# Reordering the transfers at the start of the second block, and the mirrored joins, in a fused Fourier mixing and squared-ReLU kernel

## The chip, the cores and the metric

The kernel runs on one core of one Trainium2 chip. A core has a matrix engine (TensorE, PE in the profile, with its weight loads listed as PEld), a vector engine (VectorE, DVE), a scalar engine (ScalarE, ACT), a general engine (GpSimd, POOL) and SP, which here only issues transfers (DMAs). Each engine works through its own list of instructions in order, and semaphores make one wait for another. The metric is the device time of one execution in microseconds (us), the median of several runs; lower is better.

## The reference

Two parts, both in float32. The first mixes a batch of 8 sequences of 3008 tokens with 256 features by a two-dimensional Fourier transform and keeps the real part. The second takes every token through two matrices with a squared ReLU between them.

```python
def _attn_ref(x):                       # x: (8, 3008, 256)
    X = np.fft.fft(x, axis=1)
    X = np.fft.fft(X, axis=2)
    return X.real.astype(np.float32)

def _moe_ref(x, w_in, w_out):           # x: (24064, 256), w_in: (256, 2048), w_out: (2048, 256)
    h = x @ w_in
    r = np.maximum(h, 0.0)
    g = r * r
    return (g @ w_out).astype(np.float32)
```

## The kernel before

**What is computed, and from what.** The transform over the tokens is done as products with tables of cosines and sines, after x has been folded (sums and differences of rows that share a table row). The result for one sequence is held as three pieces: P and Q, two arrays of 128 rows by 1505 columns (names `Pt` and `Qt`), and E, one row of 1505 numbers, the column of features that belongs to neither. The transform over the features is folded into the first matrix: G1 and G2 are w_in multiplied by the tables of that transform, `gE` the part of it that goes with E. So h = G1 P + gE E + G2 Q for one column and, with a minus in front of G2 Q, for its mirror image, which is why one step makes both.

**Steps and blocks.** The 1505 columns of a sequence are cut into six blocks of up to 252 columns, and the 2048 hidden features into 16 chunks, taken two at a time: eight steps to a block, 48 to a sequence, numbered through as `i`, with `j = i % 8`. A step is: products of G1 with P and G2 with Q on PE (`hP`, `hQ`, L1028; in steps 0 to 9 `ph`, L999 and L1001, one half of the step at a time); on VectorE E times gE added to hP (L1032; L1014 in steps 0 to 9), then sum and difference with hQ into `g` (L1036 and L1037; L1016 and L1017); on ScalarE ReLU (L1041) and square (L1044) in place. Two steps together then go through the second matrix by a scheme with fewer products: GpSimd makes sums of `g` (`s`, L1056 to L1073), and PE multiplies `g` and `s` with w_out and sums of it (`F` and `S`, L1093). The first block does the second product without that scheme (`mA`, `mB`, L1122). The sums of w_out (`wsum`) are made while steps 6 to 11 run: `copy_wout` has ScalarE copy a quarter into PSUM (`sw`, L397) and `sum_wout` has VectorE add from it (L404).

**The order.** Nothing is scheduled by a planner. Steps 0 to 9 run in the order of the tokens in ORDER, each a name for one piece of work: `f9a` are the products of step 9's first half, `d9a` the VectorE work on them, `rl` and `sq` the ReLU and square, `cm` the sums on GpSimd, `bk` the second product, `sc2b` and `su2b` the copy and the sums of one part of w_out, `PW`, `H`, `PR` the steps that bring a weight from float64 to float32. From step 10 on a loop does the same step by step; pieces of the next sequence's folding and transform are placed beside the steps, from step 12 on.

**The row of E and the transfers.** Each block needs its 252 values of E on all 128 partitions. For the first block a product spreads them (`spread_e`). For the second, token `spl` has GpSimd store the lower part of E to DRAM (`store_lower`, L989) and SP load it back, broadcast, as `ew` (`load_window`, L977). The upper part is stored by SP (`store_upper`, L992) once the mirrored joins of Q are done. `lc` issues column loads (`load_columns`, L470): single columns of x for sequences 1 to 7, from which GpSimd later makes the rows of E of those sequences; a bare `lc` issues four, `lc1` one. `load_later` issues the load of one x tile of a later sequence (`xt`, L183, or L174 in pieces of 32 rows); its first three stand in the code at the first `f` token of step 8. GpSimd takes the difference of the first two tiles at token `df` (L605), ahead of the sums of step 8. All transfers from SP go out in the order of the code, and an issue that waits holds those behind it.

**Mirrored joins.** P and Q of sequence 0 are joined from even and odd parts. The lower columns (0 to 752) are joined before and in the first block. The upper, mirrored columns come from four joins (`join_hi`; L801 for Q, L811 for P), which `rows_at(i)` places at the end of the steps from `HI_AT` on. Block three (columns 504 to 755), which starts at step 16, is the first that needs one of them. `load_window` for the third block stands at step `HI_AT + 2`.

**PSUM.** The tiles `ph`, `hP`, `hQ` and the scratch for folding (`sp`) share two buffers in turn, so a product can start only when the tile two before it has been read.

The lines of the loop that place the joins' companions:

```python
if (i == HI_AT + 2 or j == 2 and i > HI_AT) and i + NJ < len(steps):
    load_window(*steps[i - j + NJ][:3])
...
if HI_AT <= i < HI_AT + 4:
    rows_at(i)
```

Of the kernel before, what the change touches and what calls it, by code (L numbers as in the profile page):

```python
# [84 lines left out]
def kernel(  # L85
# [20 lines left out]
    NJ = NFC // 2  # L106
# [3 lines left out]
    NX = 3  # L110
# [59 lines left out]
    def load_x(b, t):  # L170
        if b and (t >= ODD0 or t == TWO + 1):
            xt[b, t] = xp.tile([P, 4, D], F32, name="xt", tag="x")
            for p, first, count, step in later_rows(t):
                nc.sync.dma_start(out=xt[b, t][p:p + count], in_=x[b, first:first + step * (count - 1) + 1:step])  # L174
            return
        c, r0, step, rows = TILES[t]

        while rows % 15 and rows % 16 and r0 + step * rows < NROW:
            rows += 1

        pool, tag = (gp, "g") if b == 0 and t < NT - NX else (xp, "x")
        xt[b, t] = pool.tile([P, 4, D], F32, name="xt", tag=tag)
        nc.sync.dma_start(out=xt[b, t][0:rows], in_=x[b, r0:r0 + step * (rows - 1) + 1:step])  # L183
# [4 lines left out]
    def load_later(i):  # L188
        if i < len(LATER):
            load_x(*LATER[i])  # L190
# [155 lines left out]
    def dft_win(j, side):  # L346

        tab, nm = ((cosd, "mC"), (sind, "mD"))[side]
        pg = psm.tile([P, CH], F32, name="pg", tag=nm) if j else psh.tile([P, CH], F32, name="pg", tag="h")
        for i in range(2):  # L350
            nc.tensor.matmul(pg, tab[:, i], win[j][:, i], start=i == 0, stop=i == 1)
        return pg
# [3 lines left out]
    def keep_win(j, side, pg):  # L356
        to, v = (G1, G2)[side].rearrange("p (h j f) -> j p h f", h=2, j=NJ)[j], pg.rearrange("p (h f) -> p h f", h=2)
        nc.scalar.mul(to, v, 1.0 / FACTOR)
        if side and j not in BY_PRODUCTS:
            nc.sync.dma_start(out=g_dram[j:j + 1].rearrange("o (h f) -> o h f", h=2),  # L360
                              in_=G2[P - 1:P].rearrange("o (h j f) -> j o h f", h=2, j=NJ)[j])

    def ends_of(j):
        ps = psd.tile([P, CH], F32, name="pe", tag="d")
        for h in range(2):
            fc = j + NJ * h
            nc.tensor.matmul(ps[:, h:h + 1], G2[:, fc * P:(fc + 1) * P], last, start=True, stop=True)
        return ps

    def keep_ends(j, ps):  # L370
        nc.vector.tensor_copy(gE[:, j::NJ], ps[:, 0:2])

    def take_ends(j):
        nc.sync.dma_start(out=gE[:, j::NJ], in_=g_dram[j].rearrange("(h f) -> f h", h=2))
# [93 lines left out]
    def load_columns(count):  # L468
        for t, i, p, first, n, step in COLUMNS[:count]:
            nc.sync.dma_start(out=xe[p:p + n, i, SPOT[t]],  # L470
                              in_=x[1:B, first:first + step * (n - 1) + 1:step, i, H].rearrange("b r -> r b"))
        del COLUMNS[:count]
# [503 lines left out]
    def load_window(b, k0, n):  # L976
        nc.sync.dma_start(out=new_window(b, k0)[:, 0:n], in_=e_dram[b:b + 1, k0:k0 + n].to_broadcast([P, n]))  # L977

    def spread_e():

        qt = PQE[0][1]
        ps = psd.tile([P, CH], F32, name="pe", tag="d")[:, 0:CK]
        nc.tensor.matmul(ps, last.to_broadcast([P, P]), qt[:, 0:CK], start=True, stop=True)
        return lambda: nc.scalar.copy(new_window(0, 0), ps)
# [3 lines left out]
    def store_lower():  # L988
        nc.gpsimd.dma_start(out=e_dram[0:1, CK:KH], in_=PQE[0][1][P - 1:P, CK:KH])  # L989
# [4 lines left out]
    def front_half(b, k0, n, j, h):  # L994

        pt, qt = PQE[b]
        ks, fs = slice(k0, k0 + n), slice((j + NJ * h) * P, (j + NJ * h + 1) * P)
        ps = psh.tile([P, 2, CH], F32, name="ph", tag="h")
        nc.tensor.matmul(ps[:, 0, 0:n], G1[:, fs], pt[:, ks], start=True, stop=True)  # L999
        rows = P if b else P - 1  # L1000
        nc.tensor.matmul(ps[:, 1, 0:n], G2[0:rows, fs], qt[0:rows, ks], start=True, stop=True)  # L1001
        return ps
# [312 lines left out]
    def p_part(*names):  # L1315
        for nm in names:
            for kp in range(2):
                groups[0, kp, nm]()

    def q_part(*names):  # L1320
        for nm in names:
            for kp in range(2):
                groups[1, kp, nm]()
# [121 lines left out]
    def piece_beside():  # L1445
# [12 lines left out]
        'PWw1 H4 bk0 PR4 TS5 Hw1 rl2 PRw1 PW5 pgD4 f3a GD4 dE4 d3b pgC4 TSw2 d3a sq2 bk1 GC4 H5 PWw2 PR5 TS6 Hw2 '  # L1458
        'PW6 PRw2 rl3 TSw3 H6 PWw3 pgD5 PR6 f4b GD5 dE5 f4a d4b sq3 pgC5 d4a bk2 GC5 rl4 TS7 Hw3 PW7 PRw3 TSw4 H7 lc1 '
        'pgC6 sc1a PWw4 su1a PR7 f5b Hw4 GC6 PRw4 pgD6 d5b sq4 f5a sc2a GD6 dE6 lc3 d5a rl5 bk3 TSw5 PWw5 su2a sq5 TSw6 '  # L1460
        'Hw5 PWw6 PRw5 pgD7 restP f6b GD7 dE7 lc Hw6 f6a PRw6 d6b sc0a pgC7 TSw7 d6a bk4 restQ GC7 PWw7 spl lc rl6 '
        'su0a Hw7 f7b PRw7 f7a sq6 sc3a d7b bk5 d7a rl7 su3a sc1b f8b sq7 f8a su1b d8b bk6 d8a rl8 sc2b su2b '
        'f9a sq8 f9b df d9a cm8 d9b rl9 sc0b sq9 bk7 cm9 '
    ).split()
    rounds = {"2": round_win(2, raw["in", 2])}
# [3 lines left out]
    def load_more():  # L1469
        while len(loaded) < len(ROUNDED) and (len(loaded) < NX + 1 or loaded[-NX - 1] in freed):  # L1470
            nm = ROUNDED[len(loaded)]
            out_, j = nm[0] == "w", int(nm[-1])
            loaded.append(nm)
            rounds[nm] = (round_wout if out_ else round_win)(j, load((pair_out if out_ else pair_in)(j)))

    def front_at(i):
        b, k0, n, j = steps[i]
        if ("g", i) not in made:
            made["g", i] = new_g()
        return b, k0, n, j, made["g", i]  # L1480

    HI_AT = NJ + 4

    def rows_at(i):
        j = i - HI_AT
        groups[j < 2, j % 2, "hi"]()
        if j % 2:
            if j == 1:
                store_upper()
# [26 lines left out]
    def step(token):  # L1516


        what, nm = re.fullmatch("([A-Za-z]+?)(w?[0-9]*[ab]?)", token).groups()
        if what in PHASES:  # L1520
            rounds[nm][PHASES.index(what)]()
            if what == "H":
                freed.add(nm)
                load_more()
        elif what == "sp":
            made["et"] = spread_e()
        elif what == "et":
            made["et"]()
        elif what == "df":
            for f in beginning:  # L1530
                f()
        elif what == "lc":
            load_columns(int(nm or 4))
        elif what == "keep":
            q_part("keep")
        elif what == "restQ":
            q_part("rest")
        elif what == "restP":
            p_part("rest")
        elif what == "spl":  # L1540
            store_lower()
            load_window(0, *BLOCKS[1])
        elif what in ("pgC", "pgD"):
            made[what, nm] = dft_win(int(nm), int(what == "pgD"))
        elif what in ("GC", "GD"):
            keep_win(int(nm), int(what == "GD"), made["pg" + what[1], nm])
        elif what == "fe":
            made["fe", nm] = ends_of(int(nm))
        elif what == "gE":
            keep_ends(int(nm), made["fe", nm])  # L1550
        elif what == "dE":
            take_ends(int(nm))
        elif what in "fd":
            i, h = int(nm[:-1]), int(nm[-1] == "b")
            if what == "f":
                if i >= NJ and ("x", i) not in made:
                    made["x", i] = True
                    if i == NJ:
                        for k in range(NX):
                            load_later(k)  # L1560
                    load_columns(4)
                made[token] = front_half(*steps[i], h)
            else:
                split_half(*steps[i], h, front_at(i)[-1], made["f" + nm])
        elif what in ("rl", "sq"):
            (relu if what == "rl" else square)(steps[int(nm)][2], made["g", int(nm)])
        elif what == "cm":
            sums_of(int(nm))
        elif what in ("sc", "su"):
            (copy_wout if what == "sc" else sum_wout)(int(nm[0]), int(nm[1] == "b"))  # L1570
        elif what == "hi":
            rows_at(int(nm))
        else:
            assert what == "bk"
            back_at(int(nm))

    side = ahead(1)
    i = 0
# [17 lines left out]
    for i in range(PLAIN, len(steps) + 2):  # L1596
        if i < len(steps):
            b, k0, n, j = steps[i]
            if i % per == 0:
                assert not side and not composites  # L1600
                side = ahead(b + 1) if b + 1 < B else []
                spent, pace = 0.0, sum(t for t, _ in side) / sum(share(i + k) for k in range(per - 2))
            if (i == HI_AT + 2 or j == 2 and i > HI_AT) and i + NJ < len(steps):
                load_window(*steps[i - j + NJ][:3])
# [55 lines left out]
        free_pieces()  # L1660
        if HI_AT <= i < HI_AT + 4:
            rows_at(i)
# [66 lines left out]
```

## Time and profile before

| what | value |
|---|---|
| median of the runs | 1868.86 us (1868.69, 1868.86, 3262.93) |
| profiled execution, whole | 1869.89 us |
| its span, first to last instruction | 1868.1 us |
| mean granted TensorE clock | 0.999 |
| VectorE, ScalarE, GpSimd busy | 79%, 58%, 78% of the span |
| transferred | 69.52 MB, mean 37 GB/s |
| PE on the chain that ended last | 93% |

The profile is one execution. Times in its views are us from the span's start; a line of the timeline gives start, length, engine, line of the code, operation, output and input, shape and count, and in square brackets how long the engine idled before it and what ended that. A line of waits gives the sum, the number and the longest. A line of windows gives, for a stretch, its length, the busy time and count of PE, PEld, DVE, ACT and POOL, the granted clock, the share of the DMA engines' time and GB/s. The steady part is regular: from 300 us on two steps take 9.10 us of PE without a gap. What is not regular lies in the first 250 us, where weights, tables and the first sequence are made ready, and in the last 10 us.

### The profile page before, as it was taken

The numbers are of one execution on the slowest core, as the hardware profiler recorded it, in microseconds if no ns is written. First come the engines' busy times: TensorE is split into PE (matmuls) and PEld (weight loads), VectorE is DVE, ScalarE is ACT, GpSimd is POOL, SyncE is SP. The second block draws the span as 40 slices with busy tenths as digits, with TensorE's granted clock in tenths as the row PEclk, the third lists the DMA queues.
The fourth block names the chain that finished last, engine by engine and source line by source line (L and its number), as shares of the span: only waits on it lengthen the run. The fifth ranks groups of instructions, "written<-read, shape, count | busy, mean of one in ns | idle before, by whom it ended". The sixth has DMA issues, their size and how long they took to land.

```text
span 1868.1 us, 33982 instructions
## 1 busy us (share of the span) xinstructions
PE 1855.5 (99%) x11368; PEld 1752.2 (94%) x11368; DVE 1476.6 (79%) x3483; ACT 1075.0 (58%) x1592; POOL 1461.3 (78%) x2137
## 2 busy tenths in 40 slices
PE   9999999999999999999999999999999999999999
PEld 7589999999999999999999999999999999999998
DVE  8888787887788877878787887788878888766666
ACT  4776555666465655566556574566645656444454
POOL 4399778878787887888778887788877878788885
PEclk9999999999999999999999999999999999999999
DMA  7431001100011111111011110111001100000010
GB/s 204 113 56 46 15 22 47 50 23 21 20 52 40 29 23 32 31 46 30 17 32 45 37 27 15 39 51 36 15 19 41 40 15 20 16 23 15 20 44 23
DMA packets 153541, 69.52 MB, mean 37 GB/s; under 512 B 132851, under 2 KB 144601, under 8 KB 153368
## 3 DMA queue, kind: packets, MB, share of 16 engines
q1 hardware_dynamic: 152822, 66.80, 14.3%
q8 instruction: 91, 1.49, 0.3%
q14 instruction: 82, 0.67, 0.1%
q0 software_dynamic: 416, 0.43, 0.1%
q10 hardware_dynamic: 130, 0.12, 0.0%
HBM read 42.60 MB, written 24.69 MB: 36 GB/s over the span
## 4 chain that ended last, share of the span: by engine, by line
PE 93%; DVE 1%; ACT 0%; issue 0%; DMA 0%; SPq 0%; DVEq 0%; ACTq 0%
PE F L1093 33%; PE S L1093 23%; PE hQ L1028 17%; PE hP L1028 17%; PE pd L881 1%; PE pd L855 1%; PE pd L758 1%; PE fin L1202 0%; DVE he L1032 0%; DVE Pt L811 0%; DVE g L1037 0%; DVE g L1036 0%; DVE w L658 0%; ACT sp L681 0%; DVE Qt L801 0%
## 5 line engine op out<-in xcount | busy, mean ns | idle before, releaser
L1041 ACT ACTIVATE g<-g 128x1008 f32<-128x1008 f32 (+1 forms) x384 | 399.4, 1040 | 309.9 <-DVE g L1037 282.8
L1032 DVE SCALAR_TENSOR_TENSOR he<-ew,gE,hP 128x252 f32<-128x252 f32 (+1 forms) x748 | 321.1, 471 | 287.4 <-PE hP L1028 287.2
L1044 ACT ACTIVATE g<-g 128x1008 f32<-128x1008 f32 (+1 forms) x384 | 399.4, 1040 | 11.9
L1028 PE MATMUL hP<-Pt,G 128*128 128x252 f32 (+1 forms) x1496 | 379.1, 376 | 3.0 <-DVE Pt L811 1.9
L1028 PE MATMUL hQ<-Qt,G 128*128 128x252 f32 (+3 forms) x1496 | 380.4, 377 | 1.0 <-ACT g L1041 0.5
L1093 PE MATMUL F<-s,wsum 128*128 128x168 f32 (+1 forms) x1496 | 335.5, 306 | 0.0
L1028 PEld LDWEIGHTS hQ<-Qt,G 128*128 128x128 f32 (+1 forms) x1496 | 282.1, 190 | 39.5 <-issue 2.6
L1093 PE MATMUL F<-g,wout 128*128 128x168 f32 (+1 forms) x1496 | 304.1, 305 | 0.0
L1066 POOL TENSOR_TENSOR s<-g 128x168 f32<-128x168 f32 (+1 forms) x187 | 100.8, 539 | 257.7 <-ACT g L1044 133.0
L1028 PEld LDWEIGHTS hP<-Pt,G 128*128 128x128 f32 x1496 | 265.9, 190 | 22.4 <-DVE Pt L811 2.1
L1036 DVE TENSOR_TENSOR g<-he,hQ 128x504 f32<-128x504 f32 (+1 forms) x374 | 252.7, 676 | 41.3 <-DVE he L1032 2.8
L1093 PE MATMUL S<-s,wout 128*128 128x168 f32 (+1 forms) x1496 | 280.9, 307 | 0.0
L1093 PE MATMUL S<-s,wsum 128*128 128x168 f32 (+1 forms) x1496 | 273.9, 306 | 0.0
L1093 PE MATMUL F<-g,wsum 128*128 128x168 f32 (+1 forms) x1496 | 273.5, 305 | 0.0
L1037 DVE TENSOR_TENSOR g<-he,hQ 128x504 f32<-128x504 f32 (+1 forms) x374 | 250.3, 669 | 0.0
L1093 PEld LDWEIGHTS F<-s,wsum 128*128 128x128 f32 x1496 | 247.6, 190 | 0.0
L1093 PEld LDWEIGHTS S<-s,wsum 128*128 128x128 f32 x1496 | 239.6, 190 | 8.2
L1093 PEld LDWEIGHTS F<-g,wsum 128*128 128x128 f32 x1496 | 239.3, 190 | 8.1
L1093 PEld LDWEIGHTS F<-g,wout 128*128 128x128 f32 x1496 | 239.4, 190 | 0.0
L1093 PEld LDWEIGHTS S<-s,wout 128*128 128x128 f32 x1496 | 231.7, 190 | 0.7 <-POOL s L1067 0.3
L1069 POOL TENSOR_TENSOR s<-s 128x336 f32<-128x336 f32 (+1 forms) x187 | 168.6, 902 | 14.7
L1072 POOL TENSOR_TENSOR s<-s 128x336 f32<-128x336 f32 (+1 forms) x187 | 167.6, 896 | 14.7
(221 smaller groups left out, 2484.7 us busy)
## 6 DMA issues: line engine op xcount, KB each, us to landing
out_dram<-os SPq DMA_DIRECT2D x376, 56.0 KB
xt<-in_x_dram SPq DMA_DIRECT2D x39, 384.0 KB
xt<-in_x_dram SPq DMA_DIRECT2D x63, 128.0 KB
raw<-in_moe_w_out_dram SPq DMA_DIRECT2D x20, 256.0 KB
ew<-e_dram SPq DMA_DIRECT2D x39, 126.0 KB
out_dram<-os SPq DMA_DIRECT2D x288, 7.0 KB
raw<-in_moe_w_in_dram SPq DMA_DIRECT2D x16, 256.0 KB
xt<-in_x_dram SPq DMA_DIRECT2D x2, 512.0 KB
```

The costliest lines, as they stand in the source:

```text
L758: nc.tensor.matmul(ps[0:w.shape[-1]], w, part_of(cosT if lone_e else tab, t)[0:rows, kp, PLACE[t]:PLACE[t] + NC[kp][c]], start=t == ts[0] ...
L855: nc.tensor.matmul(to, left(pair[part != which]), columns(tab, TWO, o)[0:HALF2], start=True, stop=True)
L1028: nc.tensor.matmul(to[:, h, 0:n], w[:, fs], v[:, ks], start=h == 0, stop=True, skip_group_check=True)
L1032: nc.vector.scalar_tensor_tensor(out=t[:, h, 0:n], in0=window[b, k0][:, 0:n], scalar=gE[:, fc:fc + 1], in1=hP[:, h, 0:n], op0=ALU.mult, op ...
L1036: tt(out=g[:, :, 0:n], in0=t[:, :, 0:n], in1=hQ[:, :, 0:n], op=ALU.add)
L1037: tt(out=g[:, :, n:2 * n][:, :, ::-1], in0=t[:, :, 0:n], in1=hQ[:, :, 0:n], op=ALU.subtract)
L1041: act(g[:, :, 0:2 * n], g[:, :, 0:2 * n], AF.Relu)
L1044: act(g[:, :, 0:2 * n], g[:, :, 0:2 * n], AF.Square)
L1066: gt(out=s[:, 11], in0=b2[:, 0], in1=b1[:, 0], op=SUB)
L1069: gt(out=s[:, 4:6], in0=s[:, 4:6], in1=s[:, 10:11].to_broadcast([P, 2, tb]), op=SUB)
L1072: gt(out=s[:, 6:9:2], in0=s[:, 2:4], in1=s[:, 6:8], op=ADD)
L1093: nc.tensor.matmul(acc[nm][:, slot, 0:tb], w, v, start=q == 0 and nm not in begun, stop=q == end - 1, skip_group_check=True)
```

## The change

Three edits; the instructions stay the same in number and kind on every engine.

```diff
@@ ORDER
-        'Hw5 PWw6 PRw5 pgD7 restP f6b GD7 dE7 lc Hw6 f6a PRw6 d6b sc0a pgC7 TSw7 d6a bk4 restQ GC7 PWw7 spl lc rl6 '
-        'su0a Hw7 f7b PRw7 f7a sq6 sc3a d7b bk5 d7a rl7 su3a sc1b f8b sq7 f8a su1b d8b bk6 d8a rl8 sc2b su2b '
+        'Hw5 PWw6 PRw5 pgD7 restP f6b GD7 dE7 lc1 Hw6 f6a PRw6 d6b sc0a pgC7 TSw7 d6a bk4 restQ GC7 PWw7 spl xl lc7 rl6 '
+        'su0a Hw7 f7b PRw7 f7a sq6 sc3a d7b bk5 d7a rl7 su3a sc1b f8b sq7 f8a su1b sc2b d8b bk6 d8a su2b rl8 '
         'f9a sq8 f9b df d9a cm8 d9b rl9 sc0b sq9 bk7 cm9 '
@@
-    HI_AT = NJ + 4
+    HI_AT = NJ + 3
@@ def step(token)
+        elif what == "xl":
+            for k in range(NX):
+                load_later(k)
@@
-                    if i == NJ:
-                        for k in range(NX):
-                            load_later(k)
                     load_columns(4)
```

On SP the order at this place was: four column loads of 94 rows, the row of E, four column loads of 32 rows, three x tiles, then column loads. It becomes: one column load of 94 rows, the row of E, the three x tiles, then the other three of 94 rows and the rest. On ScalarE the copy of `sc2b` stands ahead of the ReLU of step 8 instead of behind it; VectorE's order is not changed by that. With `HI_AT` at 11 instead of 12 each of the four joins stands at the end of the step before, on VectorE; and on SP the upper store of E, a group of five column loads and the third block's row of E stand ahead of the three pieces of one x tile, behind which they stood.

## The prediction

> **What bounds the kernel now.** I read the engines' busy shares first, then the matrix engine's waits over the whole span, then its timeline where those waits lie, then the SP queue, VectorE and GpSimd at the same places, then the granted clock by stretches.
>
> ```profile
> PE 1855.5 (99%) x11368; PEld 1752.2 (94%) x11368; DVE 1476.6 (79%) x3483; ACT 1075.0 (58%) x1592; POOL 1461.3 (78%) x2137
> ```
>
> ```profile
> PE hP L1028 <- DVE Pt L811: 1.9, 1, 1.9
> PE ph L999 <- DVE g L1017: 1.7, 2, 1.5
> ...
> PE hP L1028 <- DVE g L1017: 0.9, 1, 0.9
> ```
>
> PE idles 1868.1 - 1855.5 = 12.6 us in all, so nothing that shortens waits alone can bring more than 0.7 per cent. The waits listed are whole-span sums, each at one place. Those on g L1017 lie at 89 to 96 us, in steps 9 and 10 (the second block of columns begins at step 8); the one on Pt lies at 125 us, at the start of the third block. PE's timeline there, then its clock:
>
> ```profile
> 89.45 0.69 PE L999 MATMUL ph<-Pt,G 128*128 128x252 f32 x2 [1.47 <-DVE g L1017]
> ...
> 94.49 1.12 PE L1028 MATMUL hP<-Pt,G 128*128 128x252 f32 x4 [0.88 <-DVE g L1017]
> ...
> 125.06 1.21 PE L1028 MATMUL hP<-Pt,G 128*128 128x252 f32 x4 [1.88 <-DVE Pt L811]
> ```
>
> ```profile
> 126.00:127.00 1.00, 1.00 (x4) 0.77 (x3) 0.69 (x2) 0.15 (x1) 0.92 (x3) 0.50 0.27 2
> 127.00:128.00 1.00, 1.00 (x4) 0.83 (x3) 0.17 (x1) 0.71 (x2) 1.00 (x1) 0.50 0.21 2
> 128.00:129.00 1.00, 1.00 (x5) 1.00 (x5) 0.96 (x2) 0.04 (x1) 1.00 (x3) 0.50 0.00 0
> ```
>
> The first cluster, with 0.24 us each ahead of the products at 90.81 and 95.85, is 1.47 + 0.24 + 0.88 + 0.24 = 2.83 us. The second is 1.88 us of idle, and behind it the granted clock (third number from the end) stands at 0.50 for three us and at 0.82 for the next: with 0.98 just before, 3 x 0.50 + 0.18 + 0.02 = 1.70 us lost in matmuls that count as busy. The mean clock of 0.999 over the span leaves about 1.9 us for all dips, so this is nearly the only one. What makes VectorE late shows in SP's, VectorE's and GpSimd's timelines:
>
> ```profile
> 76.30 7.14 SPq L470 DMA_DIRECT2D xe<-in_x_dram  x4
> 83.54 1.94 SPq L977 DMA_DIRECT2D ew<-e_dram  x1
> ...
> 87.51 0.39 SPq L183 DMA_DIRECT2D xt<-in_x_dram  x1
> ```
>
> ```profile
> 88.14 0.48 DVE L1014 SCALAR_TENSOR_TENSOR he<-ew,gE,ph 128x252 f32<-128x252 f32 x1 [1.92 <-DMA ew<-e_dram]
> ...
> 92.19 1.09 DVE L404 TENSOR_TENSOR wsum<-sw,wout 128x256 f32<-128x256 f32 x3 [1.44 <-ACT sw L397]
> ...
> 124.38 0.63 DVE L811 TENSOR_TENSOR Pt<-dc,w 128x376 f32<-128x376 f32 x1
> ```
>
> ```profile
> 91.64 1.27 POOL L605 TENSOR_TENSOR fd<-xt 96x512 f32<-96x512 f32 x1 [9.10 <-DMA xt<-in_x_dram]
> ```
>
> Four column loads (xe, 94 rows each) hold the queue for 7.14 us, the row of E (ew) goes out behind them and VectorE waits 1.92 us for it; then 1.44 us for the copy of w_out, which ScalarE does only after the relu of step 8. The last mirrored join ends at 124.38 + 0.63 = 125.01, and PE starts at 125.06.
>
> **Part by part. The row of E.** On SP it passes three loads of 94 rows, and the four of 32 rows behind it move too. It still waits for its source: GpSimd issues that store at 78.62, and the page has 2.2 us to landing, 80.8; it cannot have landed after 83.54, when ew was issued. The load without a queue ahead is not in the trace. Bounds: 1.62 us (store to next load of g_dram, 74.24 to 75.86) and 4.13 us (the first x tile, 384 KB, 87.51 to its use at 91.64). So it lands between 82.4 and 87.7; I take 83.5, nearer the small row, as it moves 126 KB. VectorE is ready at 85.81 + 0.41 = 86.22, so the 1.92 us vanish (the late end would leave 1.5 us). Then d8b ends at 88.99 + 0.41 - 1.92 = 87.5 and PE reaches f9a at 86.98 + 1.01 = 88.0: no wait. d8a ends at 90.75 - 1.92 = 88.8, PE reaches f9b at 89.1: no wait. That is 1.71 us.
>
> **The copy of w_out** is one ScalarE copy (0.36 us, row at 91.80). Ahead of the relu it runs right after the square at 84.72, to about 86.1, in a time in which ScalarE waits 5.10 us for g; its PSUM buffer was freed at 84.4, when the weight sums before it ended. Nothing queued behind it is delayed. VectorE's three sums follow d8a at once: 88.8 + 1.09 = 89.9, d9a (1.24 us, 93.20 to 94.44) ends at 91.2, d9b at 92.5. PE comes to hP at 88.0 + 2 x 1.1 (f9a, f9b) + 1.86 (the plain products, 91.76 to 93.62) = 92.0 and to hQ at 93.0: the 0.88 and 0.24 go. Both moves together: 2.83 us. Left in place, the copy would have kept d9a until 92.6 and PE for some 0.6 us.
>
> **The x tiles** now stand behind ew on SP and wait with it, to 81 or at worst 83.5, where SP before issued column loads. GpSimd's two differences then start near 86 and 88 instead of 91.64 and 93.55, and end before the square of step 8 lets the sums begin (93.13 - 2.0 = 91.1). PE needs those sums only at 100, so this earns nothing by itself; it keeps GpSimd level with PE. The third tile takes the last weight's buffer, free at 80.9. Three 94-row loads go behind the tiles at 2.24 us each of SP time (76.66 to 78.90), and 20 others at 0.60 (9.59 us for 16): SP is done at 84.1 + 6.7 + 12.0 = 102.8 against 99.4, and its next x tile cannot go before about 104.8 (107.64 - 2.83). The columns are first read at 145.1. Cost nothing; 2 us of slack cover it.
>
> **The joins.** Four on VectorE (1.25, 1.23, 1.47, 0.63 us at 108.28, 113.86, 118.51, 124.38) go from steps 12-15 to 11-14. The first falls into VectorE's 1.31 us of waiting for PE before 104.72. The others exchange places, up to 0.24 us later at step 13 (1.47 for 1.23); hQ of step 15 hangs on that, and I charge 0.2. The last is then a step before the third block. What is late next for hP at 125.06? PE's own products end at 123.18; its PSUM buffer is freed by the fold at 122.04 + 0.68 = 122.72, that of hQ by the one ending at 123.83, before hQ's turn at 124.0. So the 1.88 us go, and, if the dip follows the gap, 1.70 us of clock. With the joins go the upper store of E and the third block's row of E, on SP now ahead of one x tile's three loads: that row went out at 118.69 and was first used at 126.31, so it has time, and the tile behind it waited for its buffer until 114.70 anyway.
>
> **GpSimd** is busy without a gap from 98.67 to 147. It follows only the first 2.83 us (it starts on the square of step 9), plus 0.90 idle at 147.06, so 3.73, while PE would be 6.41 early. The narrowest place is the S products at 185.09: their third one comes at 185.66, its sum ends at 182.65 + 0.54 = 183.19. Cover 2.47, needed 6.41 - 3.73 = 2.68: charged 0.2.
>
> Sum: 2.83 + 1.88 + 1.70 - 0.2 - 0.2 = 6.0 us. Profiled execution: 1869.89 (span 1868.1, 1.8 around it) to 1863.9. The median shown, 1868.86, is 1.03 below it, so I forecast 1862.9.
>
> **The rivals.** (1) The dip stays. For the tie of dip to gap: it is the only one and follows the longest single idle between start and end. Against: 2.83 us of gaps at 88 to 96 brought none, so the gap length is not the whole cause. If it stays, 4.3 us are gained: 1864.6. [...]
> (2) Only part is won: VectorE is busy nearly without pause from 105 to 125 us, and if the joins, crowded into steps 12-14, hold the folds back, hP of step 14 (already 0.18 late on a fold at 113.20) takes a wait of about 1.25 us (one join) and the dip comes behind it. Gain 6.0 - 1.25 - 1.70: 1865.8.
> (3) ew is no earlier, because its store lands late; the copy alone then wins little, and the x tiles wait with it. With a landing past 87.7 and the joins as in (2), about no change: 1868.5.
> (4) Slower: GpSimd cannot follow. If its sums run later than PE in steps 18 to 25, each of four pairs waits for them, in all 6.41 - 3.73 = 2.7 us, and if each wait brings a dip of 1.70: -6.0 + 2.7 + 6.8 = 3.5 us slower, 1872.4. It decides from a lateness beyond the 2.47 us of cover, which my sum misses by 0.2; against it, waits that small (0.47 at 215.54) left the clock at 1.00.
>
> **How the numbers follow.** Forecast 0.60 (own range 1861.2 to 1864.2: up to 0.7 us more if short ramps behind the gaps go too, VectorE leaving PE 3.5 early instead of 2.83), the dip stays 0.13, part won 0.14, no change 0.05, slower 0.08. The range 1861.2 to 1866.6 takes in the first three less their edges, some 0.82. Two per cent, 37 us, is about what a measurement of this kernel can tell from no change; no case reaches it: faster 0.01, within 0.97, slower 0.02.
>
> **What would show it.** Right: no wait of L1014 on ew near 86 us, no wait of L404 on the copy, L605 starting before 89, PE's idle near 7.9 us over the span, the third block's hP straight behind F, and 1.00 in every stretch to 1850. Wrong: a PE wait on a GpSimd sum between 130 and 190, a clock of 0.50 anywhere there, or hP of step 14 or 15 waiting over 0.5 us on a fold.

## The result and the profile after

| what | before | after |
|---|---|---|
| median of 7 executions each | 1868.86 us (six from 1868.55 to 1870.27, one of 3262.93) | 1862.86 us (1862.69 to 1863.26) |
| ratio, 95% interval | | 0.9966 (0.9954 to 0.9979) |
| profiled execution; its span | 1869.89; 1868.1 us | 1862.73; 1860.9 us |
| mean granted clock of that execution | 0.999 | 1.000 |

The change takes 6.0 us off, a third of a per cent: the interval lies wholly below 1, and the change is far inside two per cent. The execution of 3262.93 us, in a slower state, is not in the ratio. The profiled pair differs by 7.2 us.

The busy shares of the changed kernel, from the page: PE is still the bound, with 1860.9 - 1852.5 = 8.4 us of idle left of 12.6.

```profile
PE 1852.5 (100%) x11368; PEld 1750.9 (94%) x11368; DVE 1475.5 (79%) x3483; ACT 1075.1 (58%) x1592; POOL 1461.7 (79%) x2137
```

Its PE waits (sum, number, longest). The three lines of before, on Pt and on g L1017, are gone. A new one stands third: PE waits for a GpSimd sum.

```profile
PE filled L255 <- POOL ident masks.py:199: 1.4, 1, 1.4
PE pg L351 <- POOL win L329: 0.8, 1, 0.8
PE S L1093 <- POOL s L1073: 0.8, 1, 0.8
```

SP's timeline. The row of E is issued at 80.77 instead of 83.54, the x tiles right behind it (81.22 to 83.46); the column loads that follow hold the queue until 103.48, and the next x tile goes at 104.07.

```profile
80.77 0.35 SPq L977 DMA_DIRECT2D ew<-e_dram  x1
...
83.51 19.97 SPq L470 DMA_DIRECT2D xe<-in_x_dram  x23
```

VectorE's timeline. The first line, step 8's work on `ew`, carries no bracket now, and neither do the sums of w_out at 88.63. The last join runs from 113.86 for 0.68 us and is done 4 us before PE needs it. The second line is a new place of idleness, on the same GpSimd sum as PE.

```profile
86.11 0.47 DVE L1014 SCALAR_TENSOR_TENSOR he<-ew,gE,ph 128x252 f32<-128x252 f32 x1
...
121.59 0.68 DVE L1036 TENSOR_TENSOR g<-he,hQ 128x504 f32<-128x504 f32 x1 [1.28 <-POOL s L1073]
```

PE's timeline: steps 9 and 10 start without a wait (87.79 and 91.42), so does the third block in the first line, and then the sum of step 16 is late.

```profile
118.40 1.01 PE L1028 MATMUL hP<-Pt,G 128*128 128x252 f32 x4
...
121.61 0.84 PE L1093 MATMUL S<-s,wout 128*128 128x168 f32 x4 [0.78 <-POOL s L1073]
```

GpSimd's timeline: the first difference starts 5 us sooner than before, the second at 88.51. Behind the line at 95.10 none has a bracket up to 198 us, so the sum that PE waits for (L1073, 121.03 to 121.57) is the last of a gapless chain.

```profile
86.64 1.27 POOL L605 TENSOR_TENSOR fd<-xt 96x512 f32<-96x512 f32 x1 [4.13 <-DMA xt<-in_x_dram]
```

The granted clock (third number from the end) is 1.00 in every stretch of the steps, also in the one that holds PE's new idle time and in those behind it:

```profile
120.00:122.00 2.00, 1.22 (x8) 0.94 (x7) 0.72 (x2) 1.34 (x5) 1.87 (x3) 1.00 0.51 106
```

**Where the 7.2 us of the profiled pair come from.** The same products can be found in both timelines, and the difference of their starts read along the way (before 84 us it is 0.03):

| product | before | after | sooner by | gained since the line above |
|---|---|---|---|---|
| hP of step 10 | 94.49 | 91.42 | 3.07 | 3.07 |
| F behind step 11 | 100.20 | 96.63 | 3.57 | 0.50 |
| hP of step 14 | 113.20 | 109.29 | 3.91 | 0.34 |
| F behind step 15 | 119.60 | 114.98 | 4.62 | 0.71 |
| hP of step 16, third block | 125.06 | 118.40 | 6.66 | 2.04 |
| F behind step 17 | 132.53 | 125.39 | 7.14 | 0.48 |

Steps 8 to 11 give 3.57, steps 12 to 15 another 1.05, the start of the third block 2.04. Behind it 1.70 us of half clock should have come back and only 0.48 did, so the new wait costs about 1.2, of which 0.78 is tagged. The sum is 3.57 + 1.05 + 2.04 + 0.48 = 7.1. Two of the experiments below give the last step without the clock: with the gap but no half clock behind it (transfers alone; joins back at 12), the stretch from hP of step 16 to F behind step 17 takes 5.94 us. It takes 7.47 before and 6.99 after, so read this way the half clock cost 1.53 and the new wait 1.05.

### The profile page after: what moved, and what is told of

Read it like the earlier page. It is cut to its first block, busy times and chain, and to the rows that moved or that the text cites. A ratio compares the mean times of both kernels' runs of the same rounds, so it can differ in the third digit from the quotient of the medians.

```text
span 1860.9 us, 33983 instructions
## 1 busy us (share of the span) xinstructions
PE 1852.5 (100%) x11368; PEld 1750.9 (94%) x11368; DVE 1475.5 (79%) x3483; ACT 1075.1 (58%) x1592; POOL 1461.7 (79%) x2137
## 4 chain that ended last, share of the span: by engine, by line
PE 94%; DVE 3%; POOL 2%; ACT 1%; DMA 0%; issue 0%; SPq 0%; DVEq 0%; POOLq 0%; ACTq 0%
PE F L1093 34%; PE S L1093 23%; PE hQ L1028 17%; PE hP L1028 17%; PE pd L881 1%; PE pd L855 1%; PE pd L758 1%; DVE fd L320 1%; PE fin L1202 0%; DVE he L1014 0%; DVE w L572 0%; DVE wsum L404 0%; PE pg L351 0%; DVE g L1017 0%; DVE fs L554 0%
## 5 line engine op out<-in xcount | busy, mean ns | idle before, releaser
L1036 DVE TENSOR_TENSOR g<-he,hQ 128x504 f32<-128x504 f32 (+1 forms) x374 | 253.0, 676 | 41.0 <-DVE he L1032 1.8
```

The lines of the kernel that those rows point to most:

```text
L1036: tt(out=g[:, :, 0:n], in0=t[:, :, 0:n], in1=hQ[:, :, 0:n], op=ALU.add)
```

## The experiments

Medians are in us, the number of executions in brackets, ratios with their 95% interval; each against executions of the kernel before on the same chip (1868.94 in the first four, 1868.99 in the next four, 1869.84 in the last three of which a time counts). Those last three ran on another chip than the first eight, with no repeat of the changed kernel beside them; a difference of some tenths between them and the changed kernel is less certain than the others.

**One part alone, from the kernel before.** My theory was that each part works at its own place and the parts add up.

The copy alone:

```diff
-  'su0a Hw7 ... sc1b f8b sq7 f8a su1b d8b bk6 d8a rl8 sc2b su2b '
+  'su0a Hw7 ... sc1b f8b sq7 f8a su1b sc2b d8b bk6 d8a su2b rl8 '
```

> The kernel before with only the copy of sc2b ahead of the ReLU of step 8. Theory (each PE wait has its own last cause, gains add): VectorE still waits 1.9 us for the row of E, PE keeps 1.47 + 0.24 us at f9a and f9b, but VectorE's three sums follow d8a at once, d9a comes 1.4 us sooner, and the 0.88 and 0.24 us ahead of hP and hQ of step 10 go: about 1.1 us faster. Rival (the late row of E sets the whole cluster): nothing, within 0.3 us.

1866.33 (11; 1865.33 to 1869.60), ratio 0.9985 (0.9976 to 0.9994): 2.6 us faster, more than twice what was expected. The 0.88 and 0.24 are gone; the wait on `ew` and the 1.88 at the third block remain. The profiled execution is the slowest of the eleven, and it shows something that the one of before did not: the clock falls to half behind the first cluster as well as behind the third block's gap (stretches of 2 us; 0.79 and 0.85 in the two beside the first line).

```profile
92.00:94.00 2.00, 2.00 (x5) 1.25 (x5) 1.83 (x6) 1.24 (x2) 1.26 (x1) 0.50 1.03 201
...
126.00:128.00 2.00, 2.00 (x7) 1.64 (x6) 0.86 (x2) 0.74 (x2) 2.00 (x3) 0.50 0.25 2
```

F behind step 11 stands at 100.55, 0.35 later than before, of which 0.15 stems from ahead of 84 us and 0.42 + 1.00 + 0.30 = 1.7 from that first dip. Without them it would be 1.5 sooner, and F behind step 15 (119.26) has gained 0.69 more: 2.2 of the 2.6. The remaining 0.4 I cannot place.

The transfers alone (one column load, the row of E, the x tiles, then the columns; the other two parts as before):

```diff
-  '... dE7 lc Hw6 ... PWw7 spl lc rl6 '
+  '... dE7 lc1 Hw6 ... PWw7 spl xl lc7 rl6 '
```

> The kernel before with only the transfers reordered (row of E behind one 94-row load, then the x tiles). Theory: VectorE's wait for E goes, f9a and f9b do not wait, but the copy is still behind the ReLU, so PE still waits about 0.6 us at hP of step 10: 1.9 to 2.5 us faster. Rival (the cluster is set by the copy as much as by E): under 1 us.

1866.90 (11; 1866.63 to 1868.12), ratio 0.9989 (0.9981 to 0.9998): 2.0 us faster, as expected. The waits of step 9 are gone; those of step 10, which hang on the copy, remain in its PE waits, as does the 1.9 on Pt:

```profile
PE hP L1028 <- DVE g L1017: 0.9, 1, 0.9
```

It matters too that behind the gap of 1.89 us at the third block (124.63) the clock of this profile stays at 1.00.

The joins alone:

```diff
-    HI_AT = NJ + 4
+    HI_AT = NJ + 3
```

> The kernel before with only the joins a step sooner. Theory: the 1.88 us of PE idle ahead of the third block go, some tenths of small waits in steps 14 and 15 with them, about 2 to 3 us of idle in all; in executions of the kernel before that show the half clock behind this gap another 1.7 us go, in those that do not, none. A wait of S on the GpSimd sum L1073 in step 16 stays under 0.5 us, since PE has not run ahead by the first cluster. [...] Rival 2 (VectorE's load sets steps 12 to 16): under 1 us won, PE waits on folds instead.

1866.56 (11; 1866.40 to 1868.12), ratio 0.9986 (0.9977 to 0.9994): 2.4 us faster, as expected. But the new wait on GpSimd, which was to stay under 0.5 us here, is already in its PE timeline with 0.80; and it is in no profile in which the joins stand at 12. So it comes with the joins and not with the transfers. The profiled execution has a dip as well, behind the first cluster (1.47 us of idle at 90.38, clock 0.51 and 0.63 over 92 to 96).

```profile
126.14 0.84 PE L1093 MATMUL S<-s,wout 128*128 128x168 f32 x4 [0.80 <-POOL s L1073]
```

The three parts alone give 2.6 + 2.0 + 2.4 = 7.0 against 6.0 together; each is uncertain by about 1.7 us, so the times neither prove nor refute that they add. The traces tell more (positions taken against the products ahead of 86 us, the half clock taken off). Up to F behind step 11 the transfers gain 2.00 and the copy 1.5, and together they gain 3.54: there they add. From there to F behind step 15 the stretch takes 19.40 us before, 18.71 with the copy alone, 18.31 with the joins alone, 19.43 with copy and transfers together (joins back at 12, below) and 18.35 with all three: there the copy's gain is lost beside the transfers, and the joins bring the whole of it.

**The x tiles left where they were, in the changed kernel.** The prediction said that moving them earns nothing by itself. Here they stand at the first `f` of step 8 again, behind all eight column loads:

```diff
-  '... PWw7 spl xl lc7 rl6 '
+  '... PWw7 spl lc7 rl6 '
...
+                    if i == NJ:
+                        for k in range(NX):
+                            load_later(k)
```

> The changed kernel with the three x tiles loaded where they were before, after eleven column loads. Theory (the x tiles keep GpSimd level with PE): three 94-row loads now stand ahead of the tiles, the first difference on GpSimd starts near 94 us instead of 86.6, the sums of steps 8 to 15 run 4 to 5 us later, and PE waits for them in the S products: 1.5 to 4 us slower than the changed kernel. Rival (the tiles are hidden anyway): within 0.3 us of the changed kernel.

1868.39 (11; 1867.58 to 1869.99), ratio 0.9996 (0.9987 to 1.0004): nearly all of the gain is lost, more than I expected. SP now stands idle from 76.6 until the store has landed at 81, in a time in which it issued columns before; the seven columns held back then take 9.00 us, and the first tile goes out at 90.66 (87.51 before). In GpSimd's timeline the first difference starts at 95.33, the second at 97.45, and the sums of step 8 behind them at 98.69 instead of 91.00:

```profile
95.33 1.28 POOL L605 TENSOR_TENSOR fd<-xt 96x512 f32<-96x512 f32 x1 [12.47 <-DMA xt<-in_x_dram]
```

and PE waits for them, at F (100.14) and again at S (127.36), with a dip behind the first (0.61 and 0.53 over 100 to 104):

```profile
PE F L1093 <- POOL s L1057: 2.4, 1, 2.4
PE S L1093 <- POOL s L1073: 1.4, 1, 1.4
```

So the early row of E and the early tiles are one part. The first without the second moves the wait from VectorE to GpSimd.

**The changed kernel once more**, beside the next three:

> The changed kernel once more, beside the next three. Theory (gains of the three edits add, less what GpSimd takes back): 6.0 us faster than the kernel before, with a spread of under 1 us, since no PE gap of over 0.8 us is left behind which the clock could drop. [...]

1863.09 (5; 1862.72 to 1863.62), ratio 0.9967 (0.9954 to 0.9979): the result again, with the same wait of 0.8 us.

**The new wait: does it cost, and can it be removed?** First, the product that reads the last sum goes from third to last place in every S, so that PE gets there later:

```diff
-  ("S0", 1, (0, 1), s[:, 4]), ("S0", 2, (0, 2), s[:, 8]), ("S1", 0, (1, 0), s[:, 6]),
-  ("S1", 1, 11, s[:, 10]), ("S1", 2, 10, s[:, 3]), ("S2", 0, 7, s[:, 7]), ("S2", 1, (1, 3), s[:, 5])
+  ("S0", 1, (0, 1), s[:, 4]), ("S1", 0, (1, 0), s[:, 6]),
+  ("S1", 1, 11, s[:, 10]), ("S1", 2, 10, s[:, 3]), ("S2", 0, 7, s[:, 7]), ("S2", 1, (1, 3), s[:, 5]), ("S0", 2, (0, 2), s[:, 8])
```

> The changed kernel with the product that reads the last GpSimd sum moved from third to last of the eight S products, in every pair. Theory (in step 16 VectorE's L1036, not PE's third S product, is what holds step 17: it starts at 121.59, right when L1073 ends, and the fold that frees hP's buffer follows it at 123.53): PE's 0.78 us wait at S goes, but hP of step 17 starts no sooner, 123.6: within 0.2 us of the changed kernel. Rival (PE's own wait is the loss): 0.7 to 0.8 us faster than the changed kernel.

1863.99 (6; 1863.62 to 1864.18), ratio 0.9971: 0.9 us slower than the repeat, where the theory had no change and the rival a gain. The 0.78 becomes 0.21, yet hP of step 17 starts at 124.06 against 124.00 in the repeat: in its PE timeline the wait has gone to the fold that frees hP's buffer.

```profile
124.06 1.12 PE L1028 MATMUL hP<-Pt,G 128*128 128x252 f32 x4 [0.61 <-DVE sc L637]
```

That fold stands on VectorE behind L1036, which waits for the same GpSimd sum (1.28 us at 121.59 above). PE's wait on S has a second wait right behind it on another path; by this reading only an earlier sum would help, which no run here shows. The 0.9 us are lost elsewhere, over the whole span: against the repeat hP stands 0.04 later at 92 us, 0.10 at 262, 0.52 at 580 (behind a wait of 0.26 on the same fold, L637) and 0.93 from 1612 on.

So GpSimd should have less to do before step 16. Three tiny products of the turning factors (L425, 0.79 us together), made at step 11, go to step 16:

```diff
-        extra.update({PLAIN + 1: (take_turn, make_turn), **tables, 17: (scale_turn,),
+        tables[16] += (make_turn,)
+        extra.update({PLAIN + 1: (take_turn,), **tables, 17: (scale_turn,),
```

> The changed kernel with three small GpSimd products for the turning factors (0.79 us at 109.93) issued at step 16 instead of 11, before their first reader at step 17. Theory (GpSimd is what is late in step 16): L1073 ends at 120.8, the wait of S is at most 0.1 us, VectorE and hP of step 17 are 0.7 to 0.8 us earlier: 0.6 to 0.8 us faster than the changed kernel. Rival (the lateness only moves on to the S products of step 18): within 0.2 us.

1864.03 (7; 1863.69 to 1864.64), ratio 0.9973: 0.9 us slower than the repeat, where theory and rival both had it faster or equal. VectorE's timeline shows why: the last join, an instruction of 0.68 us, took 2.96.

```profile
114.07 2.96 DVE L811 TENSOR_TENSOR Pt<-dc,w 128x376 f32<-128x376 f32 x1
```

GpSimd's timeline at that moment:

```profile
113.99 1.27 POOL L605 TENSOR_TENSOR fd<-xt 94x512 f32<-94x512 f32 x1
...
116.58 1.20 POOL L1068 TENSOR_TENSOR s<-g 128x336 f32<-128x336 f32 x1
```

The difference L605 had started 0.08 us before the join, and the join ended only at 117.03, behind two more GpSimd instructions (115.23 to 116.62) and with the next one, the last line, lengthened from 0.89 to 1.20. In the changed kernel the order is the other way: the join starts at 113.86, L605 at 114.09, and there it is L605 that takes longer:

```profile
114.09 1.58 POOL L605 TENSOR_TENSOR fd<-xt 94x512 f32<-94x512 f32 x1
```

The long join delays the folds behind it, and hP of step 16 waits 1.1 us on one (L619).

Both edits together:

> Both of the last two edits on the changed kernel. Theory: as the one with the turning factors, at most 0.1 us more: 0.6 to 0.9 us faster than the changed kernel. Rival (PE's wait on the sum is the loss): the same as either alone, 0.8 us.

1864.80 (11; 1864.65 to 1865.74), ratio 0.9977: 1.7 us slower than the repeat, where 0.6 to 0.9 faster was expected. The join is 2.96 us long here too; the two losses add.

**The disputed cost by itself.** Is it the two engines that lengthen each other's instructions, or the join's reversed, strided output that is slow? A kernel that computes nothing of the reference: sixteen joins alone, sixteen beside a stream of GpSimd sums, sixteen with one input in PSUM beside the same stream; `up` is a tile written every second column, backwards. Its time as a whole means nothing.

```python
for _ in range(16):
    nc.vector.tensor_tensor(out=up, in0=a, in1=b, op=SUB)      # L108, alone
...
for _ in range(16):
    nc.vector.tensor_tensor(out=up, in0=b, in1=a, op=SUB)      # L114, beside L116
for _ in range(24):
    nc.gpsimd.tensor_tensor(out=r[1], in0=g[1], in1=h, op=SUB) # L116
...
for _ in range(16):
    nc.vector.tensor_tensor(out=up, in0=a, in1=p, op=SUB)      # L119, p in PSUM, beside L121
```

> Only the disputed overlap, nothing of the reference is computed: 16 joins of 376 columns (two SBUF inputs, mirrored stride) on VectorE alone, then 16 of them beside GpSimd sums of 336 columns issued back to back, then 16 beside the same sums but with one input in PSUM. Theory (a VectorE instruction with two SBUF inputs and a GpSimd sum shut each other out): about 0.6 us each alone, over 1 us on average beside GpSimd, 0.6 to 0.7 us again with one input in PSUM; the sums, 0.9 us alone, get longer in the second part only. Rival (the long joins of 1.25 to 2.96 us have another cause, such as the stride of their output): the same time in all three parts.

The groups of instructions (count, then busy us and mean ns of one):

```profile
L114 DVE TENSOR_TENSOR o<-b,a 128x376 f32<-128x376 f32 x16 | 17.4, 1089 | 0.5
...
L108 DVE TENSOR_TENSOR o<-a,b 128x376 f32<-128x376 f32 x16 | 8.8, 550 | 0.5
L119 DVE TENSOR_TENSOR o<-a,p 128x376 f32<-128x376 f32 x16 | 8.7, 547 | 0.5
```

With the same stride a join took 0.550 alone, 1.089 on average beside the sums, and 0.547 beside them with one input in PSUM. So here it is two inputs in SBUF beside GpSimd, and not the stride. The sums pay as well: 1.020 on average (L116) for 0.892 beside the joins from PSUM (L121). But the two did not run strictly one after the other: while the 16 joins ran, from 26.21 to 44.16, some 16 sums ran too, and at the lengths they have alone that would have taken 16 x (0.55 + 0.89) = 23 us instead of 18.

**Put to use**: the turning factors at 16 as before, and ScalarE copies one input of the last join to PSUM, the form that took 0.547 beside the sums above:

```diff
+                if which == 0 and kp:
+                    held = psh.tile([P, 512], F32, name="jo", tag="h")[0:n, 0:n0]
+                    nc.scalar.copy(held, st["odd"])
+                    st["odd"] = held
```

> The kernel with the turning factors at step 16, whose last join took 2.96 us, with the kept input of that join first copied to PSUM by ScalarE. Theory (the join was shut out by GpSimd's difference, which had started 0.08 us ahead of it): the join takes 0.6 to 0.75 us, and the wait of hP in step 16 (1.1 us) shrinks or goes. Rival (the length has another cause): the join stays over 1.4 us.

1863.72 (6; 1863.43 to 1864.36), ratio 0.9969 (0.9957 to 0.9981). The join is short again, in VectorE's timeline, though it starts 0.05 us behind a GpSimd sum (115.43 to 116.32):

```profile
115.48 0.55 DVE L811 TENSOR_TENSOR Pt<-dc,jo 128x376 f32<-128x376 f32 x1 [1.31 <-ACT jo L927]
```

But it has to wait 1.31 us for the copy, which stands behind a ReLU and a square on ScalarE, and the copy takes one of the two PSUM buffers of the products: PE waits 0.8 for the join at hQ and 0.6 for a fold at hP. With 0.55 us for 2.96 the cause is confirmed; as a repair it brings nothing (0.3 us less than without the copy, on another chip).

**Two of the three turning factors at 16, one at 11**, so that the join and L605 start nearly together:

```diff
+        tables[16] += (lambda: make_turn(slice(1, 3)),)
+        extra.update({PLAIN + 1: (take_turn, lambda: make_turn(slice(0, 1))), **tables, 17: (scale_turn,),
```

> The changed kernel with two of the three turning factors at step 16 and one left at 11. Theory (who starts first, the last join or GpSimd's difference of 94 rows, decides; in the changed kernel the join is 0.23 us ahead, with all three moved 0.08 us behind): GpSimd comes some 0.2 to 0.3 us sooner there, about level with the join. If the join is first it takes 0.7 us and step 17 starts 0.3 to 0.5 us sooner than in the changed kernel, 0.3 to 0.5 us faster; if it is second it takes over 1.2 us and the kernel is 0.5 to 1 us slower. Rival (a smooth effect of GpSimd's load): in between, within 0.2 us.

1863.88 (6; 1863.68 to 1863.99), ratio 0.9969 (0.9958 to 0.9981). L605 starts at 114.06, the join at 114.10: it is second by 0.04 us, and takes 3.00 us. The kernel is 0.8 us slower than the repeat, as the theory had it for this case. The three starts of this join, 0.23 us ahead of L605 and 0.04 and 0.08 behind it, give 0.68, 3.00 and 2.96 us, nothing in between; other joins do take 1.05 to 1.47 us (118.51 before: 1.47).

**The joins back at 12, the rest changed**, for what the third block's gap costs by itself, and the dip:

```diff
-    HI_AT = NJ + 3
+    HI_AT = NJ + 4
```

> The changed kernel with the joins back at steps 12 to 15. Theory (the joins are worth the 1.88 us ahead of the third block, the small waits before it, and the half clock behind it in some executions): PE waits 1.9 us on the last join again, 2 to 2.5 us slower than the changed kernel in executions without the half clock, up to 4 us with it. Rival (the rest of the change hides the joins, since VectorE is ahead by then): under 1 us slower.

1866.62 (11; 1865.11 to 1868.31), ratio 0.9983 (0.9975 to 0.9992): 3.8 us slower than the changed kernel in the median, 3.1 by the ratios, each against the kernel before on its own chip. The gap is back, in PE's timeline:

```profile
121.78 1.12 PE L1028 MATMUL hP<-Pt,G 128*128 128x252 f32 x4 [1.89 <-DVE Pt L811]
...
127.72 0.74 PE L1093 MATMUL F<-g,wsum 128*128 128x168 f32 x4
```

The executions fall apart: three lie at 1865.11 to 1865.28, all at a mean clock of 1.000, seven at 1866.3 to 1867.5, one at 1868.31 with 0.998. The profiled one (1865.28) has the gap and no dip behind it (clock 1.00 in every stretch from 120 to 140 us). So without a dip the joins a step later cost 2.3 to 2.4 us. That is not the gap alone: against the repeat, steps 12 to 15 take 1.1 longer, the start of the third block 2.05 longer, and the new wait, which is absent here, gives 1.1 back. What lies above that, up to 3 us, I put down to dips, by the lower mean clocks alone (one of the seven has 1.000); no profile of those executions was taken.

None of these kernels is faster than the changed one.

## Why the prediction was right, and where a right number hid wrong terms

The forecast was 1862.9 and the median is 1862.86. It is right in its mechanisms; that it is right to the digit is partly luck, for four of its terms were off and the errors nearly cancel.

- **The row of E**: right. Issued at 80.77 (forecast 80.8), not waited for at 86.11, products of step 9 at 87.79 and 88.77 (88.0 and 89.1). The transfers alone took those waits away and brought 2.0 us. When the row landed no view shows, only that it was before 86.11; so the 83.5 is not tested, only its late bound.
- **The copy**: right as a part of the whole. The sums of w_out start at 88.63 (88.8), hP of step 10 at 91.42 (92.0). Alone it brought 2.6 us where 1.1 was expected: 1.5 in the first cluster, and 0.69 in steps 12 to 15 that do not last beside the transfers.
- **The first cluster's size**: under-sized, 2.83 against 3.57. The sum took only the tagged idle; 0.48 of the rest had built up by hP of step 10, 0.26 by F of step 11. Each of the four waits cost 0.14 to 0.26 more than its tag: products in a row start 0.85 us apart though each is listed with 1.01 (86.10 and 86.94), and behind the waits of before this overlap is missing (the product at 92.61 ends at 93.62, and hP starts 0.88 later, at 94.49) and the product is longer (1.12, for 1.01 at 91.42 in the changed kernel). The prediction kept this 0.7 for its range.
- **The x tiles**: the times were right (86.64 and 88.51 for 86 and 88), the SP queue too (103.5 for 102.8). "This earns nothing by itself" may hold against the kernel before (no run moves the tiles alone) and misleads as a judgment of the edit: without it the other two parts keep only 0.5 of the 6 us. The step asked what the move brings and should have asked what the early row of E does to the queue when the tiles stay behind it.
- **The joins**: the 1.88 went, 2.04 with the ramp. The charge of 0.2 for their new neighbours had the wrong sign. The four took 4.58 us together before and 3.10 after (1.09, 0.60, 0.73, 0.68), and steps 12 to 15 gained 1.05 us instead. It goes with their place: 2.95 us with the joins alone moved, 4.61 with everything but them, and the measurement by itself (0.550 alone, 1.089 beside the sums) shows that GpSimd beside them can make such a difference. The 1.05 is the joins': moved alone they gain 1.09 in that stretch, and everything but them gains nothing there (19.43 us for 19.40).
- **GpSimd**: the direction was right, the place and size wrong. I charged 0.2 at 185 us; it is 0.78 tagged and 1.05 to 1.2 in all at 121 to 124, in the S of step 16. The place at 185 was misread: other products (L758, L855) stand between the second and the third one of that S, the third starts at 186.51 and not 185.66, and the cover there was 3.32, so nothing was to be charged. At the S of step 16 GpSimd did what was forecast, its last sum 2.84 us sooner (121.03 for 123.87; forecast 2.83). PE did not: hP of step 16 came 6.66 sooner, and the forecast had 2.83 + 1.88 - 0.2 = 4.5. At 4.5 the third product of this S would have stood at about 122.8, a good 1 us behind the end of the sum it needs (an estimate: hP at 120.55, and 2.27 on, as in the profile after). So the wait follows from the two terms above, the first cluster and the joins, that were too small. Of the signs that were to show an error, a PE wait on a GpSimd sum came, ahead of the 130 to 190 named for it; PE's idle is 8.4 for 7.9. It remains far from rival 4, in which four such waits make the kernel slower, and no dip followed the wait (clock 1.00 in every stretch behind it).
- **The clock**: 1.70 us is what the profiled pair shows and not what the medians hold. Of 69 executions of the kernel before, beside the experiments, 38 lie at 1868.4 to 1869.2 and the rest at up to 1871.4: the mean clock is 0.998 in seven, all at 1869.87 or more, and 1.000 in 26, none above 1869.64. So a dip seems to go with the upper part; 0.999, in the other 36, stands in both, as a last digit of the mean clock is 1.9 us. The profiled execution, 1869.89, lies in the upper part; the median, 1868.86, in the lower. The forecast took the full 1.70 off it and, separately, started from the median. Without the clock the gains are 3.57 + 1.05 + 2.04 = 6.66 us less 1.05 to 1.2 of the wait, 5.5 to 5.6, against 5.5 to 6.3 between that lower part and 1862.86. So the 6.0 of the forecast held 1.7 that the median very likely does not have, and missed 0.74 + 1.25 + 0.16 of gains, less 0.85 to 1.0 of a wait.

Rival 1, the dip stays, fell: the twelve executions of the changed kernel lie between 1862.69 and 1863.62, eleven of them at a mean clock of 1.000. Rival 2, the folds held back by crowded joins, fell here, though it lies near: the join that started 0.04 us behind L605 took 3.00 us, and then hP of step 16 waited 1.1 us on a fold. Rival 3 fell with the row of E.

## What to carry to other kernels

Read a stall's price from where the same work stands in both timelines, and not from the tagged idle alone. When a transfer that waits for its source is moved up a queue, move up with it what others need soon, for everything behind it now waits too (here the first tile went out at 90.66 instead of 87.51). Before taking the profile's clock loss into a sum against a median, see whether the median execution has it.

## What the runs showed of the hardware

**A join with two inputs in SBUF and GpSimd instructions beside it lengthened each other, the join to as much as 3.00 us.** In the measurement by itself a join took 0.550 us alone, 1.089 on average beside GpSimd sums and 0.547 beside them with one input in PSUM; the sums took 1.020 and 0.892. In three pairs that started within 0.04 to 0.23 us, the one listed first kept its length and the other took longer: the join 0.68 us and L605 1.58 instead of 1.27 (changed kernel), or L605 1.27 and the join 2.96 (all turning factors at 16) and 3.00 (two of them at 16) instead of 0.55 to 0.7. Side by side for long they did not run strictly one after the other: 16 joins and some 16 sums passed in 18 us, and the lengths they have alone would add up to 23. In the trace with all the turning factors at 16, three GpSimd instructions ended (the last at 116.62) before the join, which is listed from 114.07, did at 117.03. Why it did not end between them no run here shows. On average over the 16 joins the loss was only 0.54 us each, so the long ones are the exception.

**Behind a short gap the half clock came in some executions and not in others.** In the steps the granted clock fell to 0.50 to 0.53 in its lowest stretch of 1 or 2 us behind idle times of PE of 1.47 us (joins alone), 1.62 and 1.87 (copy alone), 1.88 (before) and 2.42 (x tiles left); with the stretches beside it each fall lost 1.70 to 1.72 us. At the start of one execution it also fell behind 1.74 (transfers alone, at 13.33; 0.69 and 0.50 over 14 to 18 us). It stayed at 1.00 behind 1.47 (before), 1.42 (x tiles left) and 1.89 (transfers alone; joins back at 12). In the seven profiles in which no gap of the steps exceeds 1.1 us it did not come: 1.00 in every stretch read from 60 us on, in five of them to 1840 and in two (the copy to PSUM; two turning factors at 16) to 260, with a mean of 1.000 for all seven. What decides between the cases, and how the chance depends on the length of the gap, no run here shows.
